# Three query groups instead of four in a batch's edge tiles, and a whole row's pv in 64 columns

## Chip, cores and metric

The kernel runs on one core of a Trainium2 chip. The metric is the device time of one execution in microseconds.

## What is computed

A block-sparse attention (4 batches, 8 heads, 768 positions, head size 64, blocks of 32, so 24 blocks a sequence) feeds a two-layer MoE-like network. In short:

```python
scores = scale * q @ k^T                       # per batch and head
mask = |blk_i - blk_j| <= 1                    # window of three blocks
mask |= first or last block, as query or key   # dense rows and columns
mask |= 3 sampled key blocks per query block
attn = softmax(where(mask, scores, -1e9)) @ v
x = attn.transpose(0, 2, 1, 3).reshape(3072, 512)
h = maximum(x @ w_in, 0); out = (h * h) @ w_out   # 512 -> 2048 -> 512
```

The first and the last query block of a sequence attend to everything. They are called the dense query blocks; all others attend to 2 + 3 + 3 = 8 key blocks.

## The kernel before, in words

**Tiles.** A sequence is cut into six tiles of 128 rows, four query blocks ("groups" `j`) each; `order` lists the 24 tiles (batch, tile). A tile is worked on in two halves of four heads each (`Half`, u = 0 and 1). The dense query blocks are group 0 of tile 0 and group 3 of tile 5. They are computed apart by `Whole`, one per batch and pair of heads (16 in all), over all 24 key blocks. Before the change a `Half` of tile 0 or 5 computes its dense group all the same, with a window moved inside (`centre`), and only `norm` leaves it out when it writes the result.

**A half tile.** `scores` (L359) issues 32 matmuls of 64 rows by 32 columns, each run in two float32 passes: per pair of heads a window piece of 96 columns from `kn` and a piece of 160 columns from `KG` (two static blocks and three sampled ones). Group j writes PSUM partitions 32j to 32j+31. `maxima` (L382) takes the row maxima on VectorE. Tiles 0 to 5 of the order (batch 0) then run `exps`, `turn` (transposes on TensorE) and `copies` (ACT, or ACT and DVE). From tile 6 on (`MOVED`, L85) `turn_blocks` (L404) takes 16 exponentials on ACT, one per group and key block (L413), which at once move 32 rows to the partitions where a vector transpose (L418) wants them. `values` (L450) is the pv product: 32 matmuls of 128 rows by 32 columns over 65 columns of V (the 65th sums the weights); group j has its own weights and its own V columns. `norm` divides and writes x.

**A whole row.** `Whole.scores` multiplies 128 query columns (2 dense blocks of 2 heads, zeros elsewhere) by all keys, in two PSUM banks; `exps` (L557, tile name `pg`) runs on ACT; `values` (L596) has 24 matmuls of 128 rows by 32 columns, of 65 columns each, and `norm` writes four blocks of 32 rows. In QG the four column groups stand in the order (dense block i, head e).

**Loads.** `load_static`, `load_window` (L286) and `load_sampled` (L306) fill V on SyncE's queue, per half; `load_kg` (L270) fills KG there from tile 6 on, and `copy_keys` (L253) copies sampled keys on GpSimd for the first six tiles. A window load covers all neighbouring groups in one DMA. In tiles 0 and 5 the dense group's window is the same as its neighbour's, so it is a DMA of its own.

**Order.** All engines' orders are written out by hand. The 24 tiles form 8 chunks of three. Chunk 0's attention and batch 0's whole rows run first (the start). Then for each chunk the MoE matmuls (`hidden` L788, `project` L816 and L826) are emitted, and `Stream` puts pieces of the next chunk's halves and of the next batch's whole rows between them: every `yield` of `Half.run` or `Whole.run` says after how many pieces the unit goes on. In the trace s is a scores product, pv a half's value product, pvg that of a whole row, g a whole row's scores, pm the moved exponentials, ph and po the MoE products.

Of the kernel before, what the change touches and what calls it, by code (L numbers as in the profile page):

```python
# [96 lines left out]
def tile_block_sparse_attention_moe(ctx: ExitStack, tc, kd, knd, qd, qgd, vd, vnd, samp, const, wcat, out):  # L97
# [17 lines left out]
    def bank(name):  # L115
        return ps.tile([P, 512], F32, tag="s", name=name)
# [107 lines left out]

    def centre(qb):
        return min(max(qb, 1), NBLK - 2)
# [26 lines left out]
    def copy_keys(b, t, own=None):  # L253

        vals = sampled(t, 0, POOL)
        kg = keys_of(b, t, own)
        for u in range(2):
            if t < UC:
                static_keys(b, t, u, nc.gpsimd.tensor_copy)
            kn = st["kn", b, u]  # L260
            for j in range(NJ):
                for r in range(NRAND):
                    nc.gpsimd.tensor_copy(
                        kg[:, j, 2 + r, 2 * u : 2 * u + 2].unsqueeze(1), kn[:, bass.ds(vals[NRAND * j + r], 1)]
                    )
                yield
# [19 lines left out]
    def load_window(k, u, eng=nc.sync):  # L286
        us = halves(k, u)
        if us is None:
            return
        b, t = order[k]  # L290
        VB = values_of(k)[1]
        runs = []
        for j in range(NJ):
            c = centre(NJ * t + j)
            if runs and c == runs[-1][-1][1] + 1:
                runs[-1].append((j, c))
            else:
                runs.append([(j, c)])
        for run in runs:
            (j, c), n = run[0], len(run)  # L300
            for i in range(us.start, us.stop):
                src = vd[b, (c - 1) * BLK : (c + 1 + n) * BLK, i * HW // 2 : (i + 1) * HW // 2]
                src = bass.AP(src.tensor, src.offset, [[HW, 3 * BLK], [BLK * HW, n], [1, HW // 2]])
                eng.dma_start(VB[BLK:P, i, j : j + n], src)

    def load_sampled(k, u, eng, on):  # L306
        us = halves(k, u)
        if us is None:
            return
        b, t = order[k]  # L310
        VA, VB = values_of(k)
        vals = sampled(t, 1, on)
        v4 = columns(vd[b], us).rearrange("(a p) u c -> p a u c", p=BLK)
        for j in range(NJ):
            for r in range(NRAND):
                dst = VB[0:BLK, us, j] if r == 2 else VA[(2 + r) * BLK : (3 + r) * BLK, us, j]
                eng.dma_start(dst.unsqueeze(1), v4[:, bass.ds(vals[NRAND * j + r], 1)])  # L317
# [6 lines left out]
    class Half:  # L324


        def __init__(self, b, t, u):
            self.b, self.t, self.u = b, t, u
            self.k = order.index((b, t))
            self.moved = self.k >= MOVED  # L330
            self.name = f"{b}_{t}_{u}"

# [26 lines left out]
        def scores(self):  # L359
# [3 lines left out]
            for i in range(2):  # L363
                pr = 2 * u + i
                for piece in range(2):
                    for j in range(NJ):
                        c = centre(NJ * t + j)
                        for e in range(2):
# [3 lines left out]
                            else:  # L372
                                k, a, z = kg[r, j, :, pr, :], 0, S_WIN
                            nc.tensor.matmul(  # L374
                                self.sb[e][j * BLK : (j + 1) * BLK, i * NSLOT + a : i * NSLOT + z],
# [6 lines left out]
        def maxima(self):  # L382
            m = self.m = rot.tile([P, 2, 2], F32, tag="m", name=f"m{self.name}", bufs=4)
            for e in range(2):
                nc.vector.tensor_reduce(m[:, e], self.sb[e].rearrange("p (i c) -> p i c", i=2), axis=AX, op=ALU.max)  # L385
            self.p = rot.tile([P, 4, 2, NJ, BLK], F32, tag="p", name=f"p{self.name}", bufs=PBUFS)
            if not self.moved:
                nc.vector.tensor_scalar(m, m, -SCALE, None, op0=ALU.mult)
                return
            for e in range(2):  # L390
                nc.vector.tensor_tensor(  # L391
                    self.p[:, 2 * e : 2 * e + 2].rearrange("p h c a s -> p h (c a s)"),
                    self.sb[e].rearrange("p (i c) -> p i c", i=2),
                    m[:, e].unsqueeze(2).broadcast_to([P, 2, NSLOT]),
                    op=ALU.subtract,
                )
# [7 lines left out]
        def turn_blocks(self):  # L404
# [4 lines left out]
            for j in range(NJ):  # L409
                if j == 2:  # L410
                    self.next_keys()
                for a in range(NJ):
                    nc.scalar.activation(  # L413
                        p[a * BLK : (a + 1) * BLK, j], x[j * BLK : (j + 1) * BLK, :, a], AF.Exp, scale=SCALE
                    )
# [4 lines left out]
        def exps(self):  # L420
            for e in range(2):
                for i in range(2):
                    nc.scalar.activation(
                        self.p[:, 2 * e + i].rearrange("p c a s -> p (c a s)"),
                        self.sb[e][:, i * NSLOT : (i + 1) * NSLOT],
                        AF.Exp,
                        scale=SCALE,
                        bias=self.m[:, e, i : i + 1],
                    )

        def turn(self, bank):
            pt = [bank(f"pt{self.name}_{e}") for e in range(2)]
            for e in range(2):
                for i in range(2):
                    for c in range(2):
                        a = (2 * i + c) * P
                        nc.tensor.transpose(pt[e][:, a : a + P], self.p[:, 2 * e + i, c], ident)  # L437
            return pt

        def copies(self, pt):  # L440
            self.pT = rot.tile([P, NJ, 4, 2, BLK], F32, tag="pT", name=f"pT{self.name}", bufs=2)
            for e in range(2):
                src = pt[e].rearrange("p (h j q) -> p h j q", h=4, j=NJ)
                dst = self.pT[:, :, 2 * e : 2 * e + 2].rearrange("p j i c q -> p (i c) j q")
# [5 lines left out]
        def values(self, bank):  # L450
            po = bank(f"pv{self.name}")
            for i in range(2):
                for e in range(2):
                    h = 2 * i + e
                    hv = h * VW
                    for c in range(2):
                        v = values_of(self.k)[c]
                        for j in range(NJ):
                            nc.tensor.matmul(  # L459
                                po[j * BLK : (j + 1) * BLK, h * VW : (h + 1) * VW],  # L460
                                self.pT[:, j, 2 * e + i, c],
# [6 lines left out]
        def norm(self, po):  # L468
# [5 lines left out]
            nc.vector.tensor_scalar(rec, po3[:, :, D], EPS, None, op0=ALU.add)  # L474
            nc.vector.reciprocal(rec, rec)
# [31 lines left out]
    class Whole:  # L507
# [88 lines left out]
        def values(self, bank):  # L596
# [3 lines left out]
            for kt in range(NT):  # L600
                a = kt * P
                for g in range(4):
                    h = pr % 2 * 2 + g % 2
                    nc.tensor.matmul(  # L604
                        po[g * BLK : (g + 1) * BLK, :VW],
                        self.pT[:, a + g * BLK : a + (g + 1) * BLK],
# [6 lines left out]
        def norm(self, po):  # L613
# [3 lines left out]
            for g in range(4):  # L617
                i, e = divmod(g, 2)
# [394 lines left out]
```

## Time and profile before

| | |
|---|---|
| median of 3 runs | 761.54 us (760.61 to 762.57) |
| profiled execution, span from first to last instruction | 757.7 us |
| TensorE busy (matmul) | 733.0 us, 97% of the span |
| ScalarE (ACT) busy | 539.4 us, 71% |
| VectorE (DVE) busy | 500.2 us, 66% |
| GpSimd (POOL) busy | 502.1 us, 66% |
| moved by DMA | 97.45 MB |

The profiled execution's own time is listed as its span; the three runs above are whole executions, so they hold the little that lies before the first and after the last instruction as well.

How to read it: PE is TensorE's matmul, PEld its weight load, which overlaps the matmul; SP is the queue of SyncE, which issues most DMAs. A row such as `L374 PE MATMUL s<-KG,q 64*32 64x160` names the line, the engine, the operation, what is written and read, the part of the array in use (64 rows by 32 columns) and the moving operand's shape. In a timeline the first two columns are the start and the length of a merged run of like instructions, and square brackets hold the idle time of the engine before it and what ended that. A matmul's end is modelled, so intervals between starts are safer than lengths.

### The profile page before, as it was taken

Reading aid. Unit: us, or ns where it says so; the run is one execution under the profiler, and the core shown is the slowest. Engines: PE = TensorE matmul, PEld = TensorE weight load, DVE = VectorE, ACT = ScalarE, POOL = GpSimd, SP = SyncE. Lnnn points to the kernel's source line nnn. Section 1 sums busy time; section 2 is a strip of 40 time slices with the busy share of each in tenths; the row PEclk is TensorE's granted clock in tenths of the full one; section 3 lists DMA queues with packets and bytes.
Section 4 is the critical chain, followed back from the end, with each engine's and each line's share of the span. In section 5 each row is a group of like instructions: output and inputs, shape, how many; then the busy total and the mean of one; then the engine's idle time right before and its main releaser. Section 6 shows DMA issues by size and latency. Waiting matters only on the chain.

```text
span 757.7 us, 26295 instructions
## 1 busy us (share of the span) xinstructions
PE 733.0 (97%) x9832; PEld 612.4 (81%) x9832; DVE 500.2 (66%) x988; ACT 539.4 (71%) x1193; POOL 502.1 (66%) x636
## 2 busy tenths in 40 slices
PE   5779999999999999999999999999999999999997
PEld 2666777678888888888888888887888888888986
DVE  5785785658785756667777575666868666645452
ACT  5896877898876876689786767679876776733222
POOL 6963844237776675757777567666876575777885
PEclk9899999999999999999999999999999999999999
DMA  8776799644443436544434344654344352201001
GB/s 282 217 210 187 223 272 339 136 119 141 125 119 92 144 90 186 153 105 118 119 102 107 98 126 107 225 120 139 84 122 114 81 138 65 51 1 44 1 1 42
DMA packets 92434, 97.45 MB, mean 129 GB/s; under 512 B 14803, under 2 KB 79700, under 8 KB 92308
## 3 DMA queue, kind: packets, MB, share of 16 engines
q1 hardware_dynamic: 86324, 72.80, 36.6%
q0 software_dynamic: 5696, 22.58, 8.8%
q8 instruction: 78, 1.28, 0.7%
q14 instruction: 48, 0.39, 0.2%
q10 hardware_dynamic: 288, 0.39, 0.1%
HBM read 89.43 MB, written 6.29 MB: 126 GB/s over the span
## 4 chain that ended last, share of the span: by engine, by line
PE 84%; DMA 5%; ACT 5%; DVE 3%; issue 1%; SPq 1%; POOL 1%; ACTq 0%; POOLq 0%; DVEq 0%
PE ph L788 33%; PE po L826 30%; PE s L374 7%; PE pv L459 6%; DMA V<-in_v_dram 3%; PE po L816 3%; PE g L546 2%; PE pvg L604 2%; DMA KG<-in_k_dram 1%; PE pt L437 1%; PE xt L773 1%; DVE xl L777 1%; ACT V L209 1%; DMA kn<-in_kn_dram 1%; SPq L317 1%
## 5 line engine op out<-in xcount | busy, mean ns | idle before, releaser
L413 ACT ACTIVATE pm<-p 32x256 f32<-32x256 f32 x576 | 239.2, 415 | 13.2 <-DVE p L391 4.9
L788 PE MATMUL ph<-xh,wi 128*128 128x384 f32 x832 | 237.8, 347 | 0.0
L826 PE MATMUL po<-wo,gh 128*128 128x512 f32 x672 | 213.8, 399 | 0.0
L755 POOL TENSOR_TENSOR wi<-W,wi 128x512 fp32r<-128x512 f32 x104 | 142.2, 1367 | 66.8 <-DVE wi L754 35.2
L806 POOL TENSOR_TENSOR gl<-gf,gh 128x384 fp32r<-128x384 f32 x112 | 117.4, 1048 | 93.3 <-DVE gf L804 80.9
L755 POOL TENSOR_TENSOR wo<-WO,wo 128x512 fp32r<-128x512 f32 x112 | 145.8, 1301 | 49.5 <-DVE wo L754 48.6
L792 ACT ACTIVATE r<-ph 128x384 f32<-128x384 f32 x128 | 63.0, 492 | 161.6 <-PE ph L788 156.5
L804 DVE SCALAR_TENSOR_TENSOR gf<-ph,r 128x384 f32<-128x384 f32 x112 | 62.3, 556 | 150.7 <-ACT r L792 137.1
L788 PEld LDWEIGHTS ph<-xh,wi 128*128 128x128 f32 x832 | 150.4, 188 | 13.4 <-issue 7.4
L826 PEld LDWEIGHTS po<-wo,gh 128*128 128x128 f32 x672 | 123.5, 188 | 23.0 <-issue 2.8
L788 PE MATMUL ph<-xl,wi 128*128 128x384 f32 x416 | 141.4, 340 | 0.0
L826 PE MATMUL po<-wo,gl 128*128 128x512 f32 x336 | 133.1, 396 | 0.0
L754 DVE CAST wo<-WO 128x512 fp32r<-128x512 f32 x112 | 84.3, 753 | 0.0
L788 PEld LDWEIGHTS ph<-xl,wi 128*128 128x128 f32 x416 | 78.2, 188 | 6.9 <-issue 2.9
L826 PEld LDWEIGHTS po<-wo,gl 128*128 128x128 f32 x336 | 63.1, 188 | 15.7 <-POOL gl L806 1.0
L385 DVE TENSOR_REDUCE m<-s 128x2 f32<-128x512 f32 x96 | 61.6, 683 | 10.6 <-PE s L374 10.2
L799 ACT ACTIVATE gh<-r 128x384 fp32r<-128x384 f32 x112 | 59.0, 527 | 9.3 <-ACT r L792 0.4
L459 PEld LDWEIGHTS pv<-V,pT 128*32 128x32 f32 x3072 | 47.2, 109 | 18.9 <-issue 10.5
L459 PE MATMUL pv<-V,pT 128*32 128x65 f32 x3072 | 56.0, 221 | 4.4 <-ACT pT L446 2.3
L788 PE MATMUL ph<-xh,WI 128*128 128x384 f32 x192 | 54.4, 344 | 0.8 <-ACT xh L776 0.8
L374 PE MATMUL s<-KG,q 64*32 64x160 f32 x1536 | 51.3, 307 | 0.6 <-issue 0.3
L418 DVE STREAM_TRANSPOSE pT<-pm 128x1024 f32<-128x1024 f32 x36 | 44.6, 1238 | 4.9 <-ACT pm L413 4.7
(89 smaller groups left out, 933.9 us busy)
## 6 DMA issues: line engine op xcount, KB each, us to landing
craw<-in_w_dram POOLq DMA_DIRECT2D x32, 512.0 KB, 6.0
V<-in_v_dram SPq DMA_DIRECT2D x504, 32.5 KB, 1.8
KG<-in_k_dram SPq DMA_DIRECT2D x216, 64.0 KB, 2.0
V<-in_v_dram SPq DMA_DIRECT2D x28, 390.0 KB, 4.3
q<-in_q_dram SPq DMA_DIRECT2D x24, 256.0 KB, 3.6
out_dram<-ot SPq DMA_DIRECT2D x22, 256.0 KB, 2.6
V<-in_v_dram SPq DMA_DIRECT2D x16, 292.5 KB, 4.0
vn<-in_vn_dram SPq DMA_DIRECT2D x5, 780.0 KB, 6.2
```

Source lines behind the costliest of these rows:

```text
L374: nc.tensor.matmul(self.sb[e][j * BLK : (j + 1) * BLK, i * NSLOT + a : i * NSLOT + z], q[r, j, pr, :], k, start=True, stop=True,)
L385: nc.vector.tensor_reduce(m[:, e], self.sb[e].rearrange("p (i c) -> p i c", i=2), axis=AX, op=ALU.max)
L413: nc.scalar.activation(p[a * BLK : (a + 1) * BLK, j], x[j * BLK : (j + 1) * BLK, :, a], AF.Exp, scale=SCALE)
L459: nc.tensor.matmul(po[j * BLK : (j + 1) * BLK, h * VW : (h + 1) * VW], self.pT[:, j, 2 * e + i, c], v[:, self.u, j, hv : hv + VW], start=( ...
L754: nc.vector.tensor_copy(w[:, 0], src)
L755: nc.gpsimd.tensor_tensor(w[:, 1], src, w[:, 0], op=ALU.subtract)
L788: nc.tensor.matmul(ph[:, :TOK], w, x, start=(i == 0), stop=(i == len(steps) - 1))
L792: nc.scalar.activation(r, ph[:, :TOK], AF.Relu)
L799: nc.scalar.activation(gh, r, AF.Square)
L804: nc.vector.scalar_tensor_tensor(gf, ph[:, :TOK], 0.0, r, op0=ALU.max, op1=ALU.mult)
L806: nc.gpsimd.tensor_tensor(gl, gf, gh, op=ALU.subtract)
L826: nc.tensor.matmul(acc[c][u], g[:, at], w[:, k], start=(f == 0 and i == 0), stop=(f == NF - 1 and i == 2))
```

## The change

The halves of a batch's tiles 0 and 5 leave out the dense group: three groups of four in these. `groups(t)` gives the list, and `copy_keys`, `load_kg`, `load_sampled`, `scores` and `values` go over it. The remaining groups are packed into column groups 0 to 2, so that 96 partitions are in use. In tile 0 the groups stand in the order 2, 3, 1, and `norm` writes rows 64 to 127 from partitions 0 to 63 and rows 32 to 63 from partitions 64 to 95. The moved exponentials of the missing group are left out, and `yield NJ` keeps the step count. Loads and key copies for the missing group go too, and the window is then a single DMA.

In the whole rows the columns of QG are put in the order (head e, dense block i), so that the two blocks of one head are neighbours, and `values` multiplies 64 columns at a time: 12 matmuls instead of 24.

```diff
+    def groups(t):
+        return (2, 3, 1) if t == 0 else tuple(range(NJ - 1 if t == NT - 1 else NJ))
...
-            for j in range(NJ):
+            for j in sorted(groups(t)):
...
-        runs = []
-        for j in range(NJ):
-            c = centre(NJ * t + j)
-            if runs and c == runs[-1][-1][1] + 1:
-                runs[-1].append((j, c))
-            else:
-                runs.append([(j, c)])
-        for run in runs:
-            (j, c), n = run[0], len(run)
+        js = sorted(groups(t))
+        j, c, n = js[0], NJ * t + js[0], len(js)
...
+            self.js = groups(t)
+            self.rows = slice(0, len(self.js) * BLK)
...
-                    for j in range(NJ):
+                    for g, j in enumerate(self.js):
...
-                                self.sb[e][j * BLK : (j + 1) * BLK, i * NSLOT + a : i * NSLOT + z],
+                                self.sb[e][g * BLK : (g + 1) * BLK, i * NSLOT + a : i * NSLOT + z],
...
-            for j in range(NJ):
-                if j == 2:
+            for g in range(NJ):
+                if g == 2:
                     self.next_keys()
+                if g >= len(self.js):
+                    yield NJ
+                    continue
...
-            nc.vector.transpose(self.pT.rearrange("p j h c q -> p (j h c q)"), p.rearrange("p j x s -> p (j x s)"))
+            n = len(self.js)
+            nc.vector.transpose(
+                self.pT[:, :n].rearrange("p j h c q -> p (j h c q)"), p[:, :n].rearrange("p j x s -> p (j x s)")
+            )
...
-            whole = {0: ((BLK, 2 * BLK), (2 * BLK, P)), NT - 1: ((0, P - BLK),)}
-            for at in (slice(*r) for r in whole.get(t, ((0, P),))):
-                nc.vector.tensor_tensor(x3[at], po3[at, :, 0:D], rec3[at], op=ALU.mult)
+            parts = ((2 * BLK, 0, 2 * BLK), (BLK, 2 * BLK, 3 * BLK)) if t == 0 else ((0, 0, at.stop),)
+            for to, a, z in parts:
+                nc.vector.tensor_tensor(x3[to : to + z - a], po3[a:z, :, 0:D], rec3[a:z], op=ALU.mult)
...
             for kt in range(NT):
-                a = kt * P
-                for g in range(4):
-                    h = pr % 2 * 2 + g % 2
+                for e in range(2):
+                    h = pr % 2 * 2 + e
+                    a = kt * P + e * D
                     nc.tensor.matmul(
-                        po[g * BLK : (g + 1) * BLK, :VW],
-                        self.pT[:, a + g * BLK : a + (g + 1) * BLK],
+                        po[e * D : (e + 1) * D, :VW],
+                        self.pT[:, a : a + D],
                         vn[:, kt, h * VW : (h + 1) * VW],
...
-                i, e = divmod(g, 2)
+                e, i = divmod(g, 2)
...
-        qg[:, e, :, :, :, e] = q6[:, e]
+        qg[:, e, :, :, e] = q6[:, e]
```

`maxima`, `exps`, `turn` and `copies` of a half work on `self.rows` (96 partitions) or on three quarters of the columns in the same way.

More of the change, by code (lines that the diff above doesn't have):

```diff
@@ L273, in load_kg @@
         k4 = kd[b].rearrange("p (a c) -> p a c", a=NBLK)
-        for j in range(NJ):
+        for j in sorted(groups(t)):
             for r in range(NRAND):
@@ L291, in load_window @@
         VB = values_of(k)[1]
[L292 to L304 removed]
+        js = sorted(groups(t))
+        j, c, n = js[0], NJ * t + js[0], len(js)
+        for i in range(us.start, us.stop):
+            src = vd[b, (c - 1) * BLK : (c + 1 + n) * BLK, i * HW // 2 : (i + 1) * HW // 2]
+            src = bass.AP(src.tensor, src.offset, [[HW, 3 * BLK], [BLK * HW, n], [1, HW // 2]])
+            eng.dma_start(VB[BLK:P, i, j : j + n], src)
     def load_sampled(k, u, eng, on):
@@ L313, in load_sampled @@
         v4 = columns(vd[b], us).rearrange("(a p) u c -> p a u c", p=BLK)
-        for j in range(NJ):
+        for j in sorted(groups(t)):
             for r in range(NRAND):
@@ L432, in turn @@
             pt = [bank(f"pt{self.name}_{e}") for e in range(2)]
+            n = self.rows.stop
             for e in range(2):
```

42 lines of the change are left out of this document (23 added, 19 removed).

## Prediction

> **What bounds the kernel now.** I read the page's first lines, then a table of stages, then the groups of instructions, and last the timeline of single engines around the edited lines.
>
> ```profile
> span 757.7 us, 26295 instructions
> PE 733.0 (97%) x9832; PEld 612.4 (81%) x9832; DVE 500.2 (66%) x988; ACT 539.4 (71%) x1193; POOL 502.1 (66%) x636
> ```
>
> ```profile
> 0.00:20.00 20.00, 10.42 (x104) 6.00 (x108) 10.22 (x38) 10.89 (x16) 13.58 (x62) 1.00 0.87 271
> 20.00:40.00 20.00, 15.05 (x492) 11.75 (x484) 16.03 (x48) 17.28 (x40) 19.44 (x68) 0.83 0.77 226
> 40.00:57.80 17.80, 15.12 (x483) 12.09 (x476) 14.17 (x31) 17.69 (x38) 10.41 (x33) 0.90 0.74 213
> ...
> 250.00:340.00 90.00, 90.00 (x1147) 77.97 (x1147) 57.76 (x109) 67.45 (x154) 58.22 (x54) 1.00 0.50 138
> 340.00:430.00 90.00, 88.94 (x1312) 75.73 (x1311) 66.64 (x136) 70.89 (x165) 62.89 (x69) 1.00 0.42 109
> ...
> 516.00:605.00 89.00, 88.23 (x1311) 75.47 (x1310) 66.23 (x135) 70.57 (x165) 62.62 (x69) 1.00 0.42 107
> ```
>
> The columns are the stretch, its length, then busy time of PE, weight loads, DVE, ACT and POOL. There are two regimes. Up to 57.8 us (batch 0's first three tiles and its whole rows) TensorE idles and ScalarE is the engine without gaps: 17.28 of 20 and 17.69 of 17.8. After that TensorE is the bound: 90.00 of 90.00 between 250 and 340, with about 1 us missing only in 340 to 430 and 0.77 in 516 to 605, the stretches that hold the change of batch. So after 57.8 us an edit is worth what it takes off TensorE's own stream plus the gaps that it closes; work saved on ACT, DVE, POOL or SP is worth nothing by itself.
>
> **How the small matmuls run on TensorE.** The edit takes away a quarter of the scores and pv matmuls in 16 of 48 half tiles, and half of the whole rows' pv matmuls. What that is worth depends on whether they run one after another or side by side.
>
> ```profile
> L459 PE MATMUL pv<-V,pT 128*32 128x65 f32 x3072 | 56.0, 221 | 4.4 <-ACT pT L446 2.3 <-DVE ct L720 1.7
> L816 PE MATMUL po<-WO,gp 128*128 128x512 f32 x96 | 44.6, 599 | 0.0
> ```
>
> ```profile
> 66.37 2.57 PE po L816 x6
> ```
>
> ```profile
> 182.55 1.12 PE L459 MATMUL pv<-V,pT 128*32 128x65 f32 x64
> 183.59 0.40 PE L374 MATMUL s<-kn,q 64*32 64x96 f32 x16
> 183.78 0.48 PE L374 MATMUL s<-KG,q 64*32 64x160 f32 x16
> 184.06 0.37 PE L374 MATMUL s<-kn,q 64*32 64x96 f32 x16
> 184.22 0.58 PE L374 MATMUL s<-KG,q 64*32 64x160 f32 x16
> 184.74 0.50 PE L826 MATMUL po<-wo,gh 128*128 128x512 f32 x1
> ```
>
> Six records of 512 float32 columns take 2.57 us on the chain, so a record streams at 2.57/3072 = 0.84 ns a column, and one of 65 columns needs 54 ns. A pv has 64 records (32 matmuls in two passes each). One after another they would take 64 x 54 ns = 3.5 us; from 182.55 to the next start at 183.59 is 1.04 us, near the 16 x 54 ns = 0.87 us of a single column group. So the four groups of 32 columns run side by side, and a pv without one of them still has 16 rounds. The same holds for the scores: one of their eight tiles (2 row halves by 4 column groups) has 4 records of 96 and 4 of 160 columns, 1024 x 0.84 = 0.86 us, and all eight together take 184.74 - 183.59 = 1.15 us. Most of what the change leaves out on TensorE was therefore free. I price pv at 0.
>
> **Where the scores do pay.** The last sixteen KG records take 0.52 us to the next start, the first sixteen 0.28. pv's end costs 1.04 - 0.87 = 0.17 of such a tail, so some 0.07 is unexplained. The weight loads show it:
>
> ```profile
> 183.70 0.24 PEld L374 LDWEIGHTS s<-KG,q 64*32 64x32 f32 x16
> ...
> 184.14 0.34 PEld L374 LDWEIGHTS s<-KG,q 64*32 64x32 f32 x16
> ```
>
> The first sixteen spread over 0.24 us, the last over 0.34: late in a scores block the records arrive more slowly than the tiles take them. With 48 records instead of 64 that tail is not reached, which is worth 0.07 to 0.10 us. I take 0.10, for the fourteen such blocks behind the start (both halves of tile 5 of batch 0, and of tiles 0 and 5 of batches 1 to 3): 1.4 us. Six full scores blocks stand behind a shortened pv, whose sixteen missing records let theirs come earlier; between 0 and 0.10 each, I take 0.05, so 0.3. Together **1.7 us**, bounds 0 and 2.0.
>
> **Whole rows' pv.** Twelve rounds of four tiles of 32 columns become twelve rounds of two tiles of 64.
>
> ```profile
> 180.13 0.89 PE L604 MATMUL pvg<-vn,pTg 128*32 128x65 f32 x48
> 180.95 0.62 PE L788 MATMUL ph<-xh,wi 128*128 128x384 f32 x2
> ```
>
> ```profile
> L788 PEld LDWEIGHTS ph<-xh,wi 128*128 128x128 f32 x832 | 150.4, 188 | 13.4 <-issue 7.4 <-DVE x L623 0.8 <-ACT r L792 0.3
> L459 PEld LDWEIGHTS pv<-V,pT 128*32 128x32 f32 x3072 | 47.2, 109 | 18.9 <-issue 10.5 <-ACT pT L446 6.0 <-DVE x L623 1.6
> ```
>
> It takes 0.82 us, of which 48 records on four tiles = 12 rounds x 54 ns = 0.65 are streaming; the 65 moving columns do not change. A load of 32 columns lasts 109 ns and one of 128 columns 188, 0.82 ns a column, so 64 columns occupy 53 ns: just inside a round, if two tiles load side by side as four do now (48 loads of 109 ns could not fit in 0.82 us otherwise). I price it at **0**, bounds a loss in a rival below and a gain of half, 0.41 us in each of 12 behind the start.
>
> **The gap at the change of batch.**
>
> ```profile
> 342.21 0.35 PE L374 MATMUL s<-kn,q 64*32 64x96 f32 x2
> 343.32 0.31 PE L374 MATMUL s<-kn,q 64*32 64x96 f32 x7 [0.77 <-ACT pg L562]
> ...
> 344.45 0.45 PE L788 MATMUL ph<-xh,wi 128*128 128x384 f32 x1
> ```
>
> ```profile
> 328.19 0.49 ACT L792 ACTIVATE r<-ph 128x384 f32<-128x384 f32 x1 [1.15 <-PE ph L788]
> ...
> 329.32 0.84 ACT L413 ACTIVATE pm<-p 32x256 f32<-32x256 f32 x2
> ...
> 330.54 0.41 ACT L413 ACTIVATE pm<-p 32x256 f32<-32x256 f32 x1
> ...
> 331.32 0.41 ACT L413 ACTIVATE pm<-p 32x256 f32<-32x256 f32 x1
> ...
> 333.73 0.49 ACT L792 ACTIVATE r<-ph 128x384 f32<-128x384 f32 x1
> ...
> 342.58 1.05 ACT L562 ACTIVATE pg<-g,mg 128x512 f32<-128x512 f32 x2
> ```
>
> ```profile
> 332.00 0.34 PE L788 MATMUL ph<-xh,wi 128*128 128x384 f32 x1
> ```
>
> These scores take 2.24 us instead of 1.15: their PSUM bank is held until the whole row's exponentials (342.58) have read it, and ACT comes to those late because it has no gap after 328.19. Counting back in program order, the four pm rows (329.32 to 331.32, 1.66 us) are the last group of the first half of batch 2's tile 0: exactly what is left out. What is late next is ACT's r at 333.73. Its matmul ends at 332.34, so of 1.66 us some 333.73 - 332.34 = 1.39 are kept; the exponentials then end near 342.3 where the scores arrive at 342.2, and nearly the whole 1.09 us closes. The 0.77 us missing in 516 to 605 is the next batch's same place. **2.2 us**, bounds 0 (if r or the casts behind it do not move) and 2.8.
>
> **The start.** Here ACT is the chain.
>
> ```profile
> 30.84 0.65 PE L604 MATMUL pvg<-vn,pTg 128*32 128x65 f32 x13 [2.14 <-issue]
> ```
>
> ```profile
> 32.62 0.59 ACT L446 COPY pT<-pt 128x512 f32<-128x512 f32 x1 [2.05 <-PE pt L437]
> ```
>
> ```profile
> L446 ACT COPY pT<-pt 128x512 f32<-128x512 f32 x18 | 10.3, 617 | 2.8 <-PE pt L437 2.8
> ```
>
> ```profile
> q8 instruction: 78, 1.28, 0.7%
> ```
>
> Four pT copies (two halves of tile 0) shrink by a quarter of their 617 ns at most: 0.6, I take 0.5. ACT's one large gap, 2.05 us, comes from a stop of TensorE in the fourth whole row's pv for which the profile knows no releaser. I read it as the instruction stream (its queue moved 78 packets, 1.28 MB, so 16 KB each) running dry while the transfers are at 0.77; three whole rows with 48 and two scores blocks with 32 instructions fewer (loads and matmuls, 208 in all) stand ahead of that place, so it comes later or not at all, or another one opens earlier. Between a loss of 1 us and a gain of 2, I take 0.7. **1.2 us** for the start.
>
> The Trainium skill (Runtime: NRT & Kernel Launch, Instruction fetch mechanics) says that the next page of instructions is fetched while the current one runs and that crossing is mostly hidden; the 2.14 us speak against "hidden" in this stretch, if code is its cause.
>
> **What costs nothing.** Twelve halves lose four pm activations of 0.42 us on ACT: beside TensorE, except as above. SP issues 3 loads fewer per V half and per KG, and one window load fewer per half; POOL copies six keys fewer in two tiles; the vector transpose is a quarter shorter. All lie under TensorE's full rows. No wait is added: the three-group loop yields as many steps as before, so nothing shifts in the written order, and the row permutation of the whole rows moves no instruction.
>
> **The sum.** 1.7 + 0 + 2.2 + 1.2 = 5.1 us off the profiled span of 757.7. The three runs (760.61 to 762.57, median 761.54) lie 2.9 to 4.9 above that span, and nothing outside it changes: 761.5 - 5.1 = **756.4 us**. A difference of 0.3%, 2.3 us, is about what a measurement of this kernel can tell from none.
>
> **Rivals.**
> - *Only whole rounds count.* The late weight loads are a consequence of the drain, not of the number of records; the scores save nothing and 2.2 + 1.2 = 3.4 remain: 758.1. For it: 0.86 + 0.17 of the block's 1.15 us are streaming and tail. Against: the loads' 0.34 beside 0.24. Chance 0.14. The Trainium skill (TensorE: Matmul & The Clock Gate, Measured speedup vs the span model) says the same: a packed group lasts one matmul plus about 4 ns per further tile; by that, too, a missing tile would save almost nothing.
> - *ACT's freed time is lost again* in the wait for r or for the casts of the next chunk; the gaps stay: 5.1 - 2.2 = 2.9, 758.6. Against: r's matmul ends 1.39 us ahead of r. Chance 0.13. Both together: 1.2 remain, 760.3, chance 0.08.
> - *Slower: the two 64-column loads do not run side by side.* Then a round of the whole rows' pv is 2 x 53 = 106 ns instead of 54, as soon as the pair exceeds a round: 12 rounds x 0.052 = 0.62 us in each of 16 whole rows. Twelve stand on TensorE's full stretch, 7.5 us, and I count half of the start's 2.5: 756.4 + 8.7 = 765.1, more if the loads' 135 ns count in full. No 64-column tile is in this trace; four loads side by side speak against. Chance 0.08.
> - *The change does what its words say:* the cost is per matmul and the whole rows' pv halves, 12 x 0.41 = 4.9 more: 751.5. The rounds speak against. Chance 0.05.
>
> **How the numbers follow.** My forecast has 0.52. Its own spread is 753 (start and gaps at their upper bounds) to 759. The range 752.8 to 760.3 takes in the first rivals and leaves out the slow one and the halved one. Faster by over 0.3% (under 759.3): most of the forecast 0.49, of the first rival 0.11, of the second 0.10, and the last 0.05, so 0.75; slower (over 763.8): 0.08; the rest 0.17.
>
> **What would show it.** Right: pv with 48 records still 1.03 to 1.04 us; scores with 48 records 1.04 to 1.08; whole rows' pv with 24 records 0.80 to 0.82; the waits for pg at the second and third change of batch gone; TensorE's first MoE matmul 0.5 to 2.5 us earlier. Wrong: a whole row's pv above 0.9 us, scores unchanged, a new gap on TensorE between 57 and 690 us, or a start that is later.

## The result and the profile after

The changed kernel takes 753.13 us (median of 4 executions, 753.09 to 754.62); the kernel before, in executions beside it, 761.44 us (760.61 to 762.57). The ratio is 0.9899, with a 95% interval of 0.9875 to 0.9923. That is 8.3 us less, where 5.1 were predicted. A few executions below ran at a granted clock of 0.75 to 0.85 and took 810 to 900 us; no number here contains them.

The first lines of the page of after:

```profile
span 751.4 us, 24184 instructions
...
PE 726.4 (97%) x8936; PEld 608.1 (81%) x8936; DVE 497.4 (66%) x988; ACT 518.8 (69%) x1145; POOL 500.4 (67%) x624
```

The two profiled spans differ by 757.7 - 751.4 = 6.3 us. The changed kernel's profiled execution took 753.14 us, 1.8 above its span (751.37 in the finer times of the trace). A second profile of the unchanged kernel (first experiment) took 758.93 with a span of 757.16, so 1.8 there too. What lies outside the span did not change. By that, the first profile of before, with 757.7, took some 759.4 us, 2.0 under the median of 761.44: a quick one of its kind. So 6.3 of the 8.3 us are in the two traces, and the rest is how far the profiled execution of before lay under its median.

**Where the 6.3 us lie.** The first matmul of the MoE's transposes (xt) marks the end of the start: 57.51 us before, 55.04 after. That is 2.5 us. From there each chunk is the time to the next chunk's first xt, and chunk 7 the time to the start of the last matmul (from the trace):

```
         start | chunk 0      1      2      3      4      5      6      7
before   57.51 |   98.67  92.09  83.90  92.52  83.90  91.82  80.32  72.55
after    55.04 |   98.14  91.80  83.48  91.07  83.48  91.38  80.09  72.55
```

Chunks 0 to 7 together give 3.8 us (predicted: 1.7 + 2.2 = 3.9). The table of stages of after, in the columns used before; the changes of batch now begin at 338.48 and 513.04, so the last two rows are moved to hold them:

```profile
20.00:40.00 20.00, 15.84 (x457) 12.84 (x457) 16.91 (x49) 19.47 (x46) 19.44 (x67) 0.92 0.79 238
40.00:55.30 15.30, 10.72 (x400) 8.70 (x379) 13.02 (x30) 15.25 (x32) 10.26 (x32) 1.00 0.81 220
250.00:340.00 90.00, 89.96 (x1155) 77.78 (x1154) 56.55 (x109) 63.53 (x144) 60.13 (x55) 1.00 0.49 135
...
337.00:427.00 90.00, 89.96 (x1191) 77.06 (x1190) 66.13 (x135) 69.91 (x163) 63.44 (x70) 1.00 0.41 106
511.00:600.00 89.00, 88.69 (x1184) 75.80 (x1183) 66.20 (x134) 68.89 (x161) 62.95 (x69) 1.00 0.40 106
```

The two regimes are the same: ScalarE without gaps in the start, TensorE full behind it. TensorE misses 0.04 us in the stretch with the second change of batch, where it missed 1.06, and 0.31 in the one with the third, where it missed 0.77. ScalarE is busy 19.47 of 20 where it had 17.28.

**The small matmuls.** Two stretches of TensorE's timeline of after, first a shortened pv and a shortened scores block, then a whole row's pv:

```profile
306.66 1.11 PE L470 MATMUL pv<-V,pT 128*32 128x65 f32 x48
307.70 0.38 PE L373 MATMUL s<-kn,q 64*32 64x96 f32 x12
...
308.74 0.50 PE L838 MATMUL po<-wo,gh 128*128 128x512 f32 x1
```

```profile
176.76 0.92 PE L616 MATMUL pvg<-vn,pTg 128*64 128x65 f32 x24
177.60 0.62 PE L800 MATMUL ph<-xh,wi 128*128 128x384 f32 x2
```

From start to start pv takes 1.04 us with 48 records, as with 64. Scores take 1.04 instead of 1.15 (1.140 in the finer times of the trace, 1.039 now). The whole row's pv takes 0.84 (0.849 in the finer times) instead of 0.82 (0.818): half the records, and 0.03 us longer. Its weight loads, as one group of like instructions (columns: busy time, mean ns of one, idle time before them and what ended most of it):

```profile
L616 PEld LDWEIGHTS pvg<-vn,pTg 128*64 128x64 f32 x384 | 13.1, 142 | 9.1 <-ACT pTg L604 4.5 <-issue 4.0 <-DVE pTg L606 0.7
```

A load of 64 columns lasts 142 ns; twenty-four of them one after another would need 3.4 us, and the pv takes 0.85. So the loads overlap: in the finer times the two of a round start 0.007 us apart, and the rounds follow each other every 0.058 us.

**The change of batch.** TensorE's timeline at the second and at the third change, and ScalarE's ahead of each:

```profile
338.48 0.71 PE L373 MATMUL s<-kn,q 64*32 64x96 f32 x9
...
340.00 0.44 PE L800 MATMUL ph<-xh,wi 128*128 128x384 f32 x1
```

```profile
513.04 0.35 PE L373 MATMUL s<-kn,q 64*32 64x96 f32 x2
513.69 0.31 PE L373 MATMUL s<-kn,q 64*32 64x96 f32 x7 [0.30 <-ACT pg L574]
...
514.81 0.44 PE L800 MATMUL ph<-xh,wi 128*128 128x384 f32 x1
```

```profile
328.04 0.42 ACT L418 ACTIVATE pm<-p 32x256 f32<-32x256 f32 x1 [1.00 <-DVE p L393]
...
338.14 1.05 ACT L574 ACTIVATE pg<-g,mg 128x512 f32<-128x512 f32 x2
...
504.69 0.53 ACT L811 ACTIVATE gh<-r 128x384 fp32r<-128x384 f32 x1 [0.37 <-POOL wo L767]
```

The wait for pg (0.77 at both places before) is gone at the second change and 0.30 at the third. The scores there take 1.52 and 1.78 us (in the finer times) instead of 2.24 each, so 0.7 and 0.5 came back instead of 1.1 twice. ScalarE no longer has the four pm rows, but now it stands idle for 1.00 us ahead of the next half's first pm, until VectorE has written p. At the third change it has a second such wait, 0.37 us ahead of gh, for GpSimd's wo.

**The start.** The one stop of TensorE without a releaser that is left in after's start, from the timeline:

```profile
31.26 1.14 PE L470 MATMUL pv<-V,pT 128*32 128x65 f32 x41 [0.43 <-ACT pT L457]
33.05 0.33 PE L470 MATMUL pv<-V,pT 128*32 128x65 f32 x7 [0.65 <-issue]
```

The 2.14 us in the fourth whole row's pv are gone, and with them ScalarE's gap of 2.05; the 0.65 us that stand in the first half's pv now make no gap on ScalarE. The only one that it has between 18 and 56 us is 0.31, ahead of a cast of chunk 0.

### The profile page after: what moved, and what is told of

Its sections match the earlier page's. It is cut to its first block, busy times and chain, and to the rows that moved or that the text cites. A ratio compares the mean times of both kernels' runs of the same rounds, so it can differ in the third digit from the quotient of the medians.

```text
span 751.4 us, 24184 instructions
## 1 busy us (share of the span) xinstructions
PE 726.4 (97%) x8936; PEld 608.1 (81%) x8936; DVE 497.4 (66%) x988; ACT 518.8 (69%) x1145; POOL 500.4 (67%) x624
## 2 busy tenths in 40 slices
DMA packets 85786, 92.95 MB, mean 124 GB/s; under 512 B 13539, under 2 KB 73060, under 8 KB 85668
## 3 DMA queue, kind: packets, MB, share of 16 engines
q8 instruction: 71, 1.16, 0.7%
## 4 chain that ended last, share of the span: by engine, by line
PE 87%; ACT 6%; DVE 2%; DMA 2%; issue 1%; SPq 1%; ACTq 0%; POOL 0%; DVEq 0%; POOLq 0%
PE ph L800 34%; PE po L838 30%; PE s L373 6%; PE pv L470 6%; PE po L828 4%; PE g L558 2%; PE pvg L616 2%; DMA V<-in_v_dram 1%; PE xt L785 1%; ACT pm L418 1%; ACT V L217 1%; ACT V L209 1%; DMA kn<-in_kn_dram 1%; PE pt L447 1%; ACT p L432 1%
## 5 line engine op out<-in xcount | busy, mean ns | idle before, releaser
L418 ACT ACTIVATE pm<-p 32x256 f32<-32x256 f32 x528 | 219.2, 415 | 15.7 <-DVE p L393 8.2
L385 DVE TENSOR_REDUCE m<-s 128x2 f32<-128x512 f32 (+1 forms) x96 | 61.5, 682 | 8.3 <-PE s L373 8.0
L373 PE MATMUL s<-KG,q 64*32 64x160 f32 x1408 | 48.3, 301 | 0.7 <-ACT KG L288 0.7
L766 DVE CAST wi<-W 128x512 fp32r<-128x512 f32 x91 | 47.6, 523 | 0.0
```

The lines of the kernel that those rows point to most:

```text
L373: nc.tensor.matmul(self.sb[e][g * BLK : (g + 1) * BLK, i * NSLOT + a : i * NSLOT + z], q[r, j, pr, :], k, start=True, stop=True,)
L385: nc.vector.tensor_reduce(m[at, e], self.sb[e][at].rearrange("p (i c) -> p i c", i=2), axis=AX, op=ALU.max)
L418: nc.scalar.activation(p[a * BLK : (a + 1) * BLK, g], x[g * BLK : (g + 1) * BLK, :, a], AF.Exp, scale=SCALE)
L766: nc.vector.tensor_copy(w[:, 0], src)
```

## The experiments

All of these ran apart from the first comparison, on one chip. There the kernel before took 759.6 us (median; between 757 and 766), and each ratio is against these executions of it. "Change" is the changed kernel.

**The kernel before once more**, unedited, for a second profile.

> The kernel before, unchanged, profiled a second time. The changed kernel's runs lie 1.8 us above their spans; the median of before lies 3.7 above the span of its profile. Theory: the profiled execution of before was a quick one, so here runs lie about 1.8 us above their own spans (spans 758.5 to 760.5), and what differs between executions is the start, where TensorE stops without a releaser. Rival: the change itself takes 2 us off the time outside the span; then these runs lie 3.5 to 4 us above their spans.

Measured: 759.47 us (757.48 to 763.39), ratio 1.0006 (0.9982 to 1.0029). Its chunks equal the first profile's within 0.3 us, and all behind the start takes 700.06 us against 700.15; its start is 57.10, and its TensorE has four stops without releaser in the start instead of one:

```profile
30.32 0.59 PE L604 MATMUL pvg<-vn,pTg 128*32 128x65 f32 x13 [1.70 <-issue]
45.19 0.88 PE L459 MATMUL pv<-V,pT 128*32 128x65 f32 x44 [0.24 <-issue]
49.26 0.99 PE L459 MATMUL pv<-V,pT 128*32 128x65 f32 x53 [0.52 <-issue]
54.26 0.22 PE L459 MATMUL pv<-V,pT 128*32 128x65 f32 x1 [0.66 <-issue]
```

What follows: behind the start this kernel ran the same way in both traces, and TensorE's stops in the start did not. Both are quick executions, with starts 0.4 us apart. That the 6 us between its executions lie in the start is therefore likely, not shown.

**Whole rows in 64 columns alone** (on the kernel before):

```diff
-                for g in range(4):
-                    h = pr % 2 * 2 + g % 2
+                for e in range(2):
+                    h = pr % 2 * 2 + e
...
-                        po[g * BLK : (g + 1) * BLK, :VW],
+                        po[e * D : (e + 1) * D, :VW],
...
-        qg[:, e, :, :, :, e] = q6[:, e]
+        qg[:, e, :, :, e] = q6[:, e]
```

> Before with the whole rows' part alone (64 columns, 12 matmuls). Theory: the rounds of 64 columns cost 0.03 us more in each of 16 whole rows, 0.4 to 0.5 us in all, and fewer instructions move the stop in the start: 760 to 762. Rival (half the matmuls halve the time, or this part brings the start's gain): 758 or less.

Measured: 761.43 us, ratio 1.0013 (0.9986 to 1.0040), in two groups: four executions from 756.5 to 757.4, six from 761.1 to 763.0. The profiled one is of the quick group: span 755.1, start 55.31 (2.2 us earlier than before's), chunks as before's within 0.2 us but for chunk 3 (91.90 instead of 92.52). The stop in the fourth whole row is gone there and stands in the first half's pv, with 0.51 us. What follows: this part alone gives nothing that is reliable. In the quick execution the stop is away; that the start is as long as ever in the others is not shown, for there is no trace of one.

**Half tiles in three groups alone** (the change with the whole rows left at 32 columns; the edit is the reverse of the one above).

> The change with the whole rows left at 32 columns and 24 matmuls. Theory: 0.4 to 0.5 us quicker than the changed kernel on TensorE, 752.5 to 753, with the start as there. Rival (the whole rows bring part of the gain): 754.5 or more.

Measured: 754.31 us (753.80 to 755.97), ratio 0.9927 (0.9906 to 0.9949), between the theory and the rival. Chunks 1 to 7 are the changed kernel's within 0.2 us; chunk 0 takes 99.08 against 98.14. Start 56.98, two us later than the changed kernel's, with this at its end (TensorE's timeline, then the window behind it in the columns of the table of stages):

```profile
56.45 0.59 PE L470 MATMUL pv<-V,pT 128*32 128x65 f32 x10 [1.20 <-issue]
```

```profile
56.00:60.00 4.00, 3.29 (x22) 2.77 (x21) 1.85 (x5) 1.39 (x3) 0.00 (x0) 0.57 1.07 262
```

Three more stops without releaser stand ahead of this one: 1.16 us in the third whole row's pv, 1.38 and 0.29 in scores. Only behind the first is ScalarE idle, for 0.49 us.

What follows: all of the gain behind the start is the half tiles'. With the whole rows' part the time is lower by a further 0.3 percent (0.9899 against 0.9927, intervals that overlap), though its own pv costs TensorE 0.03 us more each time. In the traces what it gives is in the start and in chunk 0 behind it, by where the stops fall.

**The four pm activations put back** (on the change, with the values of group 0; nothing reads them):

```diff
-                if g >= len(self.js):
-                    yield NJ
-                    continue
+                at = g if g < len(self.js) else 0
                 for a in range(NJ):
                     nc.scalar.activation(
-                        p[a * BLK : (a + 1) * BLK, g], x[g * BLK : (g + 1) * BLK, :, a], AF.Exp, scale=SCALE
+                        p[a * BLK : (a + 1) * BLK, g], x[at * BLK : (at + 1) * BLK, :, a], AF.Exp, scale=SCALE
```

> The change with four pm activations put back in each moved half of tiles 0 and 5 (they repeat the first group and nobody reads them). Theory: the waits for pg at the second and third change of batch come back to 1.1 us each, 1.2 us more than the changed kernel, and some 0.3 at the first: 754.3 to 754.8. Rival (the gaps shrank for another reason): 753.1 and scores there as in the changed kernel.

Measured: 753.72 us (753.39 to 757.45), ratio 0.9928 (0.9904 to 0.9952). The two changes of batch:

```profile
340.35 0.35 PE L373 MATMUL s<-kn,q 64*32 64x96 f32 x2
341.10 0.31 PE L373 MATMUL s<-kn,q 64*32 64x96 f32 x7 [0.40 <-ACT pg L572]
...
342.22 0.44 PE L798 MATMUL ph<-xh,wi 128*128 128x384 f32 x1
```

```profile
515.25 0.35 PE L373 MATMUL s<-kn,q 64*32 64x96 f32 x2
515.99 0.31 PE L373 MATMUL s<-kn,q 64*32 64x96 f32 x7 [0.39 <-ACT pg L572]
```

The time lies between the theory and the rival. What follows: the waits for pg come back, but only to 0.40 and 0.39 of 0.77, and the scores take 1.87 and 1.86 us (1.52 and 1.78 in the changed kernel, 2.24 before). By itself the run thus returns half of what the second change of batch had gained, and a fifth at the third. The traces show where the rest is. At the second change, from r to the next r, the stretch that holds the four activations, ScalarE takes 5.54 us before (328.19 to 333.73), 5.18 here and 4.81 in the changed kernel; from that second r to pg it takes 8.85 or 8.86 in all three. So the whole gain at the second change lies in that stretch. The activations put back are cheaper than those left out: three times in it an instruction starts 0.09 us before the one ahead of it has ended, where before each starts 0.01 us or more behind. At the third change the changed kernel has the same 4.80 from r to r, but 9.13 from there to pg: that is the wait for wo, which this run does not have.

**A fourth scores group, computed twice** (on the change; group 0's place in the list again, into the partitions that nothing reads):

```diff
-                    for g, j in enumerate(self.js):
+                    for g, j in enumerate((self.js + self.js)[:NJ]):
```

> The changed kernel with a fourth group put back into the scores of tiles 0 and 5 (it repeats the first group's matmuls into the free partitions; nobody reads it). Theory: scores blocks go from 1.04 back to 1.14, 14 x 0.10 = 1.4 us behind the start, spread as 0.2 or 0.4 a chunk: 754.3 to 755.5 with some shift in the start. Rival (only rounds count, the tail is the drain): 753.1 and blocks of 1.04 to 1.05.

Measured: 754.26 us (754.06 to 755.45), ratio 0.9933 (0.9913 to 0.9954). The block that the changed kernel runs from 307.70 to 308.74:

```profile
307.89 0.40 PE L373 MATMUL s<-kn,q 64*32 64x96 f32 x16
...
309.03 0.73 PE L838 MATMUL po<-wo,gh 128*128 128x512 f32 x2
```

Back at 1.14; chunks 2 and 4 take 83.88 again (before 83.90 each) instead of 83.48. What follows: the scores' price is 0.10 us a block, twelve of them where nothing else waits, and it is the whole gain of those chunks.

**A fourth pv group, computed twice** (the same edit in `values`, with `g % len(self.js)` for the weights).

> The changed kernel with a fourth group put back into the pv matmuls of tiles 0 and 5 (it repeats the first group's into the free partitions; nobody reads it). Theory: the four groups run side by side, a pv goes from 1.039 to 1.047 us, 0.1 us in all, and scores behind it stay: 753.1 to 753.7. Rival (time per record): 16 x 0.26 = 4 us more, 757.

Measured: 753.07 us (752.95 to 754.29), ratio 0.9898 (0.9868 to 0.9928). TensorE at the second change of batch, with 64 records again:

```profile
338.43 1.11 PE L470 MATMUL pv<-V,pT 128*32 128x65 f32 x64
339.47 0.68 PE L373 MATMUL s<-kn,q 64*32 64x96 f32 x9
```

1.04 us with 64 or with 48. What follows: the 256 pv records that are left out in the start and behind it are worth nothing.

**All dropped loads and key copies put back** (on the change: `range(NJ)` again in `copy_keys`, `load_kg` and `load_sampled`, and the windows in runs as before).

> The changed kernel with every load and key copy of the left-out group put back (sampled keys and V rows, the window in two DMAs). Theory: nothing waits for them, 753.1 to 753.6, chunks as in the changed kernel. Rival (the start was bound by SyncE's and GpSimd's queues): the start ends at 57 or later, 755 or more.

Measured: 753.38 us (752.73 to 757.03), ratio 0.9921 (0.9894 to 0.9948). It moves what the kernel before moved: 92427 packets and 97.33 MB, where the changed kernel has 85786 and 92.95 MB.

What follows: 4.4 MB and 6641 packets less are worth nothing in the median. At the third change of batch TensorE's scores are even shorter with them (1.51 us against 1.78), for ScalarE's wait for wo is not there; why was not separated. But four of the ten executions took 754.6 to 757.0, where the changed kernel's four reach 754.6. Whether the smaller load makes the start steadier is open.

**Small matmuls ahead of the start** (on the change; n = 16, 32, 60 or 64 of 32 by 32 elements, four instructions each with both passes and their loads, into a bank that nothing reads, where TensorE idles):

```diff
+    idle = bank("idle")
+    for n in range(60):
+        at = slice(n % 4 * BLK, (n % 4 + 1) * BLK)
+        nc.tensor.matmul(idle[at, 0:BLK], ident[:, at], ident[:, at], start=True, stop=True)
```

With 60 (240 instructions):

> The changed kernel with 60 small matmuls (120 records, 240 instructions with their weight loads) ahead of the first whole row's scores, where TensorE waits for kn anyway; nobody reads them. In all profiles so far TensorE's stops without a releaser stand at instruction 193 of a block of 256, whatever the work there is. Theory (code arrives in blocks of 256): the stop that stands at record 705 moves from the first pv to the fourth whole row's pv, as in the kernel before, ACT gets a gap there, and the start ends at 55.5 to 58 instead of 55.0: 753.5 to 756.5. Rival (the start's gain comes from the loads or copies that were dropped, or the stops belong to the work): 753.1 with the stop still in the first pv.

With 16, 32 and 64 (64, 128 and 256 instructions):

> The change with 16 small unread matmuls (32 records, 64 instructions with their loads) ahead of the first whole row's g. They take under 2 us of a TensorE that idles there. Theory 1 (a stop follows the count of instructions, and what it costs depends on the work that the page's edge falls into): a stop without releaser, if there is one in the start, stands after 193 mod 256 recorded instructions of TensorE, 64 instructions earlier in the work than in the changed kernel, so in the fourth whole row or its scores; the median moves to 753.5 to 755. Theory 2 (each added instruction delays the start in proportion, 4.7 us for 240): 753.1 + 1.25 = 754.4, and no tie to the count. Theory 3 (the start only fluctuates): 753.1 within 0.5.

> The same with 32 small matmuls (128 instructions). Theory 1: the stops stand at 193 mod 256, 128 instructions earlier in the work than in the changed kernel, in the fourth whole row's g or behind the third one's pv, and 128 earlier in every later pv; the median is not in proportion to the count: I take 754 to 757. Theory 2: 753.1 + 2.5 = 755.6. Theory 3: 753.1 within 0.5.

> The same with 64 small matmuls (256 instructions: the edges fall on the same work as in the changed kernel, one page more lies ahead). Theory 1: stops at 193 mod 256, in the same places of the work as in the changed kernel (the first pv of the side stream); if the place decides, the median is near the changed kernel's plus what the added matmuls and their page take, 753.5 to 755.5, below the 757.8 of the 240-instruction run. Theory 2: 753.1 + 5.0 = 758.1, above the run with 240. Theory 3: 753.1 within 0.5.

Measured: 753.13, 753.24, 757.82 and 758.50 us for 64, 128, 240 and 256 instructions; the ratios are 0.9908 (0.9882 to 0.9935), 0.9910 (0.9883 to 0.9937), 0.9975 (0.9948 to 1.0003) and 0.9967 (0.9941 to 0.9993). So neither "in proportion" holds (64 and 128 cost nothing) nor "the start only fluctuates" (240 and 256 cost about 5 us each). The times that I gave for the theory of blocks failed too: 240 and 256 lie above their ranges, 64 and 128 below. What holds of it is where the stops stand. The profiled executions with 240 and 256 (762.14 and 761.12) are long ones of their kind, 4.3 and 2.6 above their medians. The stops without releaser in the start, with 128, 240 and 256:

```profile
30.46 0.28 PE L373 MATMUL s<-kn,q 64*32 64x96 f32 x3 [0.84 <-issue]
35.34 0.51 PE L373 MATMUL s<-KG,q 64*32 64x160 f32 x16 [1.13 <-issue]
40.92 0.48 PE L373 MATMUL s<-KG,q 64*32 64x160 f32 x9 [0.36 <-issue]
45.96 0.27 PE L373 MATMUL s<-kn,q 64*32 64x96 f32 x2 [0.81 <-issue]
```

```profile
43.87 0.31 PE L470 MATMUL pv<-V,pT 128*32 128x65 f32 x4 [0.34 <-issue]
47.94 0.43 PE L470 MATMUL pv<-V,pT 128*32 128x65 f32 x14 [0.53 <-issue]
58.32 1.29 PE L470 MATMUL pv<-V,pT 128*32 128x65 f32 x35 [2.89 <-issue]
```

```profile
33.86 0.42 PE L470 MATMUL pv<-V,pT 128*32 128x65 f32 x9 [1.00 <-issue]
38.88 0.27 PE L470 MATMUL pv<-V,pT 128*32 128x65 f32 x2 [0.45 <-issue]
47.98 0.54 PE L470 MATMUL pv<-V,pT 128*32 128x65 f32 x22 [0.58 <-issue]
57.10 1.51 PE L470 MATMUL pv<-V,pT 128*32 128x65 f32 x43 [2.74 <-issue]
```

Counted in the trace (loads, matmuls and TensorE's semaphore instructions), all 31 stops without releaser of 0.15 us or more in the starts of the thirteen traces, quoted here or not, stand behind 193 or 194 instructions more than a multiple of 256: 705, 961, 1217 and 1473 with 128; 1473, 1729 and 1985 with 240; 961, 1217, 1729 and 1985 with 256; 705, 1473, 1729 and 1985 in the second profile of before; 705 in before's first profile and in the changed kernel; 449, 705, 961 and 1985 in the kernel with half tiles alone (one more in some cases). And each ends 1.2 to 1.7 us after a packet of the instruction queue (16 KB) has landed: in the kernel before the packet ended at 29.38 and TensorE went on at 30.84, in the changed kernel 31.62 and 33.05.

Two things in this were against my expectation. With 240 the stop in the fourth whole row did not appear, though the count put an edge there. And with 256 the edges fall on the same work as in the changed kernel, one page later, and yet the time is 5 us longer. The edge in the last pv of the start stops TensorE for 2.74 us there, and not at all in the changed kernel. The code packet before that edge came 6.4 us after the edge before it (47.98 to 54.42) where it came about 3 us after in the changed kernel (47.3 to 50.25); between 50 and 56 us the DMA share is 1.06 in the one and 0.87 in the other. That the packet waits behind the kernel's own loads is what these numbers suggest; no run separates it. The place in the code alone does not decide: TensorE's instructions in the run with the pm activations put back are those of the changed kernel, and its profiled execution (755.38) stops for 1.06 us at that same edge, 1729, whose packet came 5.4 us after the edge before it.

What makes such a stop dear shows in the windows around and behind it, first of the run with 256, then of the changed kernel:

```profile
52.66:56.07 3.41, 0.82 (x22) 0.41 (x21) 1.39 (x2) 2.56 (x5) 2.42 (x7) 1.00 1.04 304
56.07:59.48 3.41, 2.38 (x48) 2.21 (x49) 0.76 (x3) 0.00 (x0) 0.00 (x0) 0.50 1.03 317
59.48:62.90 3.42, 2.70 (x11) 1.90 (x9) 2.08 (x4) 2.28 (x4) 0.31 (x1) 0.50 0.69 162
62.90:66.31 3.41, 3.41 (x68) 2.38 (x69) 0.24 (x1) 0.00 (x0) 0.96 (x1) 0.50 0.31 62
```

```profile
56.00:66.00 10.00, 8.71 (x101) 6.53 (x99) 6.39 (x11) 5.85 (x13) 3.06 (x3) 1.00 0.74 184
```

TensorE is busy for 0.82 of the 3.41 us in which it mostly stands, and for the ten microseconds behind that the clock is granted at half, where TensorE has just become the bound. It stays at half over 2.38 and 2.70 us of work and is full again behind the first stretch that is full of work. The start ends at 58.54 (+3.5, of which the last stop is 2.74), and chunk 0 then takes 102.55 instead of 98.14 (+4.4). The 1.20 in the kernel with half tiles alone is followed by the 0.57 over 4 us shown there.

## Why the prediction was right, and where not

The time is inside the range, near its low end, and faster was right. It is 3.3 us under the forecast of 756.4: 2.0 by the median that the saving was taken off, 1.3 by the start. Of the signs that I gave, pv and the scores came out, the wait for pg is gone at one of the two places, and a whole row's pv is longer than I allowed. By the prediction's own steps:

- **pv at 0.** Right: 1.04 us with 48 or 64 records, and the run with the fourth group back is as fast.
- **Scores, 0.10 in fourteen blocks.** Right: 0.101 in the twelve of them where nothing else waits, 1.2 us. The two others stand behind waits for key copies and together come to about nothing. The 0.05 in six full blocks behind a shortened pv failed: those still take 1.14. The rival that only whole rounds count fails for the scores and holds for pv. The Trainium skill (TensorE: Matmul & The Clock Gate, Measured speedup vs the span model) has a packed group last one matmul plus about 4 ns for each further tile: pv agrees with it (1.038 us with three tiles, 1.046 with four); the scores do not (0.10 us for two tiles of eight).
- **Whole rows' pv at 0.** The loads do run side by side, so the slower rival fell, and nothing halves. But each takes 0.03 us more, 12 x 0.03 = 0.4 behind the start, above the 0.82 that I gave as the limit of "right".
- **The gaps at the change of batch, 2.2.** The mechanism was right, the size not: 0.7 + 0.5 = 1.2 at the two places. The step that failed is "of 1.66 us some 1.39 are kept": it counted only r as what is late next. The next half's first pm waits for VectorE's p, 1.00 us of idle. At the third change GpSimd's wo takes 0.37 more. That is the rival in which ScalarE's freed time is lost, in part, though by waits that it did not name. At the first change of batch another 0.36 came back (1.71 to 1.35 us of scores), which I had not counted.
- **A term that is not in the sum.** A scores block at 375 us in before, with a stop of 0.29 without releaser, took 1.88 us; its counterpart takes 1.14. I had not looked for it. The stop stands at 194 more than a multiple of 256 (10946), so by the count this too is code; in the second profile of before the block takes 1.63 and with whole rows alone 1.14. These terms (1.2 - 0.4 + 1.2 + 0.4 + 0.7 = 3.1) leave 0.7 of the 3.8 us behind the start to places too small to name. That 3.8 comes so near to the 3.9 of the prediction is luck.
- **The start, 1.2.** Mis-sized: 2.5 in the traces. The copies gave 0.42 (four of 0.59 us each became 0.48) and the stop more than the 0.7. ScalarE's gaps of 2.05 and 0.21 are gone, 2.26 of the 2.47. Not all of that is the stop itself: at the half clock behind it the eight transposes pt take 1.90 us (31.42 to 33.32), and 1.02 at the full clock (43.30 to 44.32 in the run with 128). I had set the value between a loss of 1 and a gain of 2 because the stop could open elsewhere; it did, but in the first half's pv, where ScalarE has other work. Reading it as code was right and is now shown by the count; that it depends on the amount of code alone is not so, and what sets its length stays open.
- **From the profiled span to the median.** I took the saving off the median of the runs although the profiled execution was some 2 us quicker than that median. The changed kernel's four executions lie between 753.1 and 754.6, so 753.1 is near a profiled span and 761.5 was not. In the later comparison, with the median of before at 759.6, the saving is some 6.5 us, taking the run with a fourth pv group (753.07) for the changed kernel, which was not among them.

The Trainium skill (Runtime: NRT & Kernel Launch, Instruction fetch mechanics) says that code comes in blocks of 16 KiB, 256 instructions, one ahead, and that crossing is mostly hidden. The period of 256 and the 16 KB packets agree with it; "hidden" does not hold in this start, where the small matmuls use up a block in some 4 to 7 us and stops of up to 2.9 us were measured.

## What to carry to other kernels

Before a small matmul is removed, look whether it is one of several that run side by side: the price is that of the rounds, plus what the number of records itself costs (0.10 us of 1.14 here, by the run that puts them back). Freed time on an engine that feeds the bound counts only until the next thing that this engine waits for, so list two steps of "what is late next", not one. And where a start is made of many small instructions, an edit's largest effect can be where the blocks of code end; profile it twice, and compare the start apart from the rest.

## What the hardware showed that I had not expected

- TensorE's stops for code come at fixed counts (193 or 194 more than a multiple of 256) and end 1.2 to 1.7 us after the packet has landed. The trace with a stop of 2.74 us just as TensorE became the bound is 8 us longer than the changed kernel's, and 4.4 of these lie in chunk 0, where ten microseconds at half clock came behind the stop.
- The half clock comes in pieces of one size. In the windows of before, then of after, these lost 4 x 0.43 = 1.7, 1.7 and 1.6 us of clock, against one such piece:

```profile
20.00:24.00 4.00, 4.00 (x121) 2.99 (x112) 1.92 (x8) 3.88 (x10) 3.88 (x10) 0.57 0.78 220
30.00:34.00 4.00, 3.16 (x53) 2.61 (x60) 3.65 (x14) 1.72 (x4) 4.00 (x19) 0.58 0.62 145
40.00:44.00 4.00, 3.95 (x104) 3.21 (x104) 2.85 (x8) 3.91 (x9) 1.16 (x7) 0.61 0.84 246
```

```profile
20.00:24.00 4.00, 4.00 (x80) 3.23 (x76) 1.94 (x8) 3.88 (x10) 3.83 (x9) 0.59 0.77 242
```

  At half clock 1.7 us are a piece of 3.4 us. In the clock's own records of the traces each piece lasts 3.41 us, and the ten microseconds above are 10.24, three of them. All 17 stretches at half clock in the starts follow on 3.41 us at full clock in which TensorE was busy for 0.8 to 1.75 us; where it was busy for longer, none follows (nor in four cases between 1.5 and 1.72). The Trainium skill (TensorE: Matmul & The Clock Gate, Part 1: The HAM clock gate) gives a window of about 3.4 us in which the clock is halved or not by how busy TensorE was; the length agrees. While ScalarE is the chain such a piece costs little: the run with 128 added instructions has none at all in its start and takes the same 753.2 us. Behind the start, where TensorE is the bound, it costs what the run with 256 shows.
- The executions lie closer together with both parts than with either alone: four of them between 753.1 and 754.6, against 753.8 to 756.0 with the half tiles and 756.5 to 763.0 with the whole rows. But small things undo it: with the loads or the pm activations put back single executions reach 757.0 and 757.5. Why the kernel before needs up to 6 us more in some executions stays open: none of those is among the traces.
